# Adding the residual of an MLP block on TensorE instead of VectorE and GpSimd

## The chip, the cores and the metric

The kernel runs on one core of one Trainium2 chip. The metric is the device time of one execution in microseconds, as the median of several runs. The engines appear in the rows as PE (TensorE, with PEld for its weight loads), DVE (VectorE), ACT (ScalarE), POOL (GpSimd) and SP (SyncE, which issues the DMAs).

## The reference

The input is 8 batches of 576 tokens, 8 heads of 64 elements (512 channels). Cut to what matters:

```python
attn = softmax(blockmask(q @ k.T / 8)); x = heads_joined(attn @ v)
h = x.transpose(0, 2, 1) @ U @ V                 # mixes tokens, rank 32
u = x + h.transpose(0, 2, 1)
y = u + np.maximum(u @ w_ch1, 0.0) @ w_ch2       # 512 -> 2048 -> 512
gate = sigmoid(causal_conv5(y)); out = gate * (y @ w_val) @ w_out
```

The change concerns the `u +` in the line of `y`.

## The kernel before

Products run in fp32r. To keep the accuracy of fp32, an operand is held as a high half and a low half (`uh`, `ul`; `w1hi`, `w1lo`; `hh`, `hl`), and a product is three matmuls: high by high, low by high, high by low. The helper `hi_act` (recorded at L89) rounds a tile to its high half on ACT, `lo` (recorded at L95) subtracts to get the low half on DVE or POOL.

The 4608 tokens are cut into 9 groups g of 512 columns. The MLP of a group runs in 16 slices f of the 2048 hidden channels, so one step is s = (g, f). `emit_h1` makes a slice of the hidden layer (12 matmuls at L824 into one PSUM bank, then `hh` by a relu on ACT at L852 and `hl` on DVE at L853). `emit_o` multiplies the slice by its rows of w2 (12 matmuls at L870, three for each of the four 128-channel blocks d) and adds them up over the 16 slices in four PSUM banks, `acc[0..3]`, which stay taken for the whole group. `emit_o` of a step stands after `emit_h1` of the next one. The other four PSUM banks are shared by everything else: attention scores, products with v (`pPV`, L595), the mixing and the hidden layer.

When f = 15 is done, the group's result is taken out, for each d: DVE adds `uh` to the bank (L882), POOL adds `ul` (L883), SP stores the 128x512 block to DRAM (L884). The tile `y` comes from a pool of two buffers, so the third block of a group needs the first block's store to have landed. From group 7 on other tiles are used, eight buffers of `gt`. The sums of the last group and its gate run at the end.

The attention of later batches is woven into the MLP steps. A generator yields pieces of it; `gap()`, called at fixed places in `emit_h1` and `emit_o`, runs as many pieces as the pace asks for. Among them are the mixing steps for a pair of heads: `mix_T` transposes x (`pT`, four 128-column products at L655, one of 64 rows at L663), `mix_G` multiplies by U (`pG`, L671), `mix_H` multiplies by V (`pH`, L694), adds the result to x on DVE (`xt`, L696) and writes the halves of u for a later group (`uh` on ACT, `ul` on POOL).

The halves of u have two buffers. Group g + 2 takes the buffer of group g, so `mix_H` puts a piece for group g + 2 into the list `later` until `y_done` has reached g. `flush_later` takes one piece from that list; it is called right after `y_done` is set, and in every second `gap()`.

The order of the work on PE is the one in which the program writes it (PE is scheduled by hand). The order on ACT, DVE, POOL and SP is set by the tile scheduler when the kernel is built; work under `tc.high_priority()` is put ahead. Each engine then runs its list in that order.

Of the kernel before, what the change touches and what calls it, by code (L numbers as in the profile page):

```python
# [9 lines left out]
F32R = mybir.dt.float32r  # L10
# [3 lines left out]
ALU = mybir.AluOpType  # L14
# [3 lines left out]
P = 128  # L18
# [4 lines left out]
def attn_moe_gate_kernel(ctx: ExitStack, tc: tile.TileContext, q, k, v, U, V, w1, w2, wval, convw, wout, out):  # L23
# [8 lines left out]
    ND = DM // P  # L32
    NF = DFF // P
# [49 lines left out]
    def f32(ap):  # L83
        return ap if ap.dtype == F32 else ap.bitcast(F32)

    vec, act, pool, pe, sp = nc.vector, nc.scalar, nc.gpsimd, nc.tensor, nc.sync
# [60 lines left out]
    const = ctx.enter_context(tc.tile_pool(name="const", bufs=1, side="left"))  # L147
# [13 lines left out]
    def open_mlp_psum():  # L161
        first.close()
        psum["acc"] = mlp.enter_context(tc.tile_pool(name="accp", bufs=1, space=PSUM, side="left"))
# [54 lines left out]
    ident = ac_p.tile([P, P], F32, name="ident")  # L218
    make_identity(nc, ident)
    unit = const.tile([KC, KC], F32, name="unit")  # L220
    pool.tensor_copy(unit, ident[0:KC, 0:KC])

    w1hi = w1_p.tile([P, ND, DFF], F32R, name="w1hi")
    w1lo = w1_p.tile([P, ND, DFF], F32R, name="w1lo")
# [393 lines left out]
    ut = {}  # L618
# [8 lines left out]
    def mix_pieces(b):  # L627
        t0, t1 = b * S, (b + 1) * S
        r = []
        for g, (a, n) in enumerate(groups):  # L630
            lo_t, hi_t = max(a, t0), min(a + n, t1)
            if lo_t < hi_t:
                r.append((g, lo_t - t0, hi_t - t0, lo_t - a))
        return r
# [46 lines left out]
    def mix_H(pn, i):  # L681
        pcs = mix_pieces(pn // NP)
        if i >= len(pcs):
            return
        gi, a0, a1, off = pcs[i]
        if gi >= 2 and gi > y_done[0] + 2:
            later.append((pn, i))
            return
        xt = xts[pn]
        d = pn % NP  # L690
        uh, ul = u_tiles(gi)
        w = a1 - a0
        ps = ps_p.tile([P, 512], F32, tag="a", name="pH")
        pe.matmul(ps[:, 0:w], gst[pn], vst[:, a0:a1], start=True, stop=True)  # L694
        with tc.high_priority():
            vec.tensor_tensor(xt[:, a0:a1], ps[:, 0:w], xt[:, a0:a1], op=ALU.add)  # L696
        hi_act(uh[:, d, off:off + w], xt[:, a0:a1])
        lo(pool, ul[:, d, off:off + w], xt[:, a0:a1], uh[:, d, off:off + w])

    def flush_later():  # L700
        if later and mix_pieces(later[0][0] // NP)[later[0][1]][0] <= y_done[0] + 2:
            mix_H(*later.pop(0))

    y_done = [-1]
# [111 lines left out]
    accs = {}  # L816

    def h1_sum(ps, s, d):
        g, f = divmod(s, NF)
        n = groups[g][1]  # L820
        uh, ul = ut[g]
        fs = slice(f * P, (f + 1) * P)
        for i, (w, x) in enumerate(((w1hi, uh), (w1hi, ul), (w1lo, uh))):
            pe.matmul(ps[:, 0:n], w[:, d, fs], x[:, d, 0:n], start=(d == 0 and i == 0), stop=(d == ND - 1 and i == 2))  # L824
# [12 lines left out]
    def emit_h1(s, gap):  # L837
        g, f = divmod(s, NF)
        n = groups[g][1]
        if s in h1p:  # L840
            ps = h1p.pop(s)
            h1_sum(ps, s, ND - 1)
        else:
            ps = psum["h1"].tile([P, GS], F32, tag="a" if psum["h1"] is ps_p else "h1", name="h1")
            for d in range(ND):
                h1_sum(ps, s, d)
                if d == 1:
                    gap()
        hh = h_p.tile([P, GS], F32R, tag="hh", name="hh")
        hl = h_p.tile([P, GS], F32R, tag="hl", name="hl")  # L850
        with tc.high_priority():
            act.activation(hh[:, 0:n], ps[:, 0:n], AF.Relu)  # L852
            latest[0] = vec.scalar_tensor_tensor(hl[:, 0:n], ps[:, 0:n], 0.0, f32(hh[:, 0:n]), op0=ALU.max, op1=ALU.subtract)  # L853
        gap()
        hts[s] = (hh, hl)

    def emit_o(s, gap):
        g, f = divmod(s, NF)
        t0, n = groups[g]
        if f == 0:  # L860
            if g == 0:
                open_mlp_psum()
            accs[g] = [psum["acc"].tile([P, GS], F32, tag=f"acc{d}", name=f"acc{d}") for d in range(ND)]
        acc = accs[g]
        hh, hl = hts.pop(s)
        w = w2t.pop(s)
        for d in range(ND):
            ds = slice(d * P, (d + 1) * P)
            for i, (wi, x) in enumerate(((0, hh), (0, hl), (1, hh))):
                pe.matmul(acc[d][:, 0:n], w[:, wi, ds], x[:, 0:n], start=(f == 0 and i == 0), stop=(f == NF - 1 and i == 2))  # L870
            if d == 1:
                gap()
        gap()
        if f == NF - 1:
            uh, ul = ut.pop(g)
            ys = []
            for d in range(ND):
                if pbp and g < NG - 1:
                    y = pbp["g"].tile([P, GS + HALO], F32, tag="gt", name="gt")
                else:  # L880
                    y = late["y"].tile([P, GS], F32, tag="y", name="y")
                vec.tensor_tensor(y[:, 0:n], acc[d][:, 0:n], f32(uh[:, d, 0:n]), op=ALU.add)  # L882
                pool.tensor_tensor(y[:, 0:n], y[:, 0:n], f32(ul[:, d, 0:n]), op=ALU.add)  # L883
                sp.dma_start(out=y_s[g][:, d, :], in_=y[:, 0:n])  # L884
            y_done[0] = g
            flush_later()


    wv = {}
# [110 lines left out]
    def open_pb():  # L1000
        att.close()
        split.close()
        pbp["w"] = pb1.enter_context(tc.tile_pool(name="pbw", bufs=1, side="right"))
        pbp["g"] = pb1.enter_context(tc.tile_pool(name="pbg", bufs=GBUF, side="right"))
        pbp["y1"] = pb1.enter_context(tc.tile_pool(name="pby1", bufs=1, side="right"))
        open_stage("right", 2)
        load_conv()
        load_wb(pbp["w"])
        stage.close()
        pbp["y2"] = pb1.enter_context(tc.tile_pool(name="pby2", bufs=1, side="right"))  # L1010
        if ABUF == 4:
            psum["h1"] = pb1.enter_context(tc.tile_pool(name="h1p", bufs=2, space=PSUM, side="right"))
        pbp["ps"] = pb1.enter_context(tc.tile_pool(name="pbps", bufs=2, space=PSUM, side="right"))
# [32 lines left out]
    def gap():  # L1046
        tick_count[0] += 1
        if tick_count[0] % EVERY == 0:
            flush_later()
        pace[0] += pace[1]  # L1050
        while pace[0] > 0 and pace[2] == 0:
            pace[0] -= 1.0
            r = next(stream, 2)
            if r:
                pace[2] = r
                if r == 2:
                    while later:
                        flush_later()
                    open_pb()

    gated_conv[0] = GATE0
    for s in range(NS + LAG):
        g, f = divmod(s, NF)
# [5 lines left out]
        if f == 0 and g < B:  # L1069
            while g > 0 and not pace[2]:  # L1070
                pace[0] = 1.0
                gap()
            if g > 0:
                emit_o(s - LAG, gap)
            if pace[2] != 2:
                pace[2] = 0
            aim(g)
        if s < NS:
            if g == NG - 1:
                if f == 1:  # L1080
                    load_y(0)
                    split_tiles(0, pbp["y1"])
                    load_y(1)
            if cwt:
                wait_conv[0] -= 1
                if not wait_conv[0]:
                    turn_conv()
            emit_h1(s, gap)
            load_w2(s)
            if g == NG - 1 and 4 <= f < 4 + 2 * ND:  # L1090
                g_, d = divmod(f - 4, ND)
                if g_ == 0:
                    split_y(0, d)
                emit_gate(g_, d)
        if s >= LAG and not (f == 0 and g < B):
            emit_o(s - LAG, gap)
# [54 lines left out]
```

## Time and profile before

| | before |
|---|---|
| median of 3 runs | 1516.54 us (1515.33 to 1517.08) |
| the profiled execution, its own time | 1518.09 us |
| span of the profiled execution | 1516.3 us |
| mean granted TensorE clock | 0.977 of 2.4 GHz |
| busy: PE, DVE, ACT, POOL | 94%, 72%, 46%, 23% of the span |

The span goes from the first to the last instruction of the profiled execution; its own time holds 1.8 us around it. That execution lies 1.55 us over the median of the runs. In rows of the timeline the first number is the start and the second the duration; matmuls are pipelined, so that the time that one costs PE is the distance from its start to the next start, and not its duration. A bracket at the end of a row is the idle time of the engine just before, and what ended it.

### The profile page before, as it was taken

Reading aid. Unit: us, or ns where it says so; the run is one execution under the profiler, and the core shown is the slowest. Engines: PE = TensorE matmul, PEld = TensorE weight load, DVE = VectorE, ACT = ScalarE, POOL = GpSimd, SP = SyncE. Lnnn points to the kernel's source line nnn. Section 1 sums busy time; section 2 is a strip of 40 time slices with the busy share of each in tenths; the row PEclk is TensorE's granted clock in tenths of the full one; section 3 lists DMA queues with packets and bytes.
Section 4 is the critical chain, followed back from the end, with each engine's and each line's share of the span. In section 5 each row is a group of like instructions: output and inputs, shape, how many; then the busy total and the mean of one; then the engine's idle time right before and its main releaser. Section 6 shows DMA issues by size and latency. Waiting matters only on the chain.

```text
span 1516.3 us, 20089 instructions
## 1 busy us (share of the span) xinstructions
PE 1430.9 (94%) x6664; PEld 1106.4 (73%) x6664; DVE 1088.6 (72%) x2249; ACT 703.7 (46%) x1501; POOL 349.0 (23%) x449
## 2 busy tenths in 40 slices
PE   5889899979998998999899989999999999999999
PEld 3556667667776776777677767767888888778887
DVE  7778877677787888788777878887424427399991
ACT  4676555535544554456355445544413211244432
POOL 2123333121113112211311131122014210352410
PEclk9999899989999999999999999999999999999999
DMA  6445765333342434333333424421225533213211
GB/s 121 103 100 160 229 188 177 85 103 84 94 105 82 103 90 114 87 93 84 103 83 94 97 90 97 95 93 62 88 97 195 180 125 125 98 65 102 84 70 70
DMA packets 246289, 163.56 MB, mean 108 GB/s; under 512 B 197669, under 2 KB 212261, under 8 KB 246186
## 3 DMA queue, kind: packets, MB, share of 16 engines
q1 hardware_dynamic: 246186, 162.29, 37.7%
q8 instruction: 53, 0.87, 0.2%
q14 instruction: 50, 0.41, 0.1%
HBM read 134.98 MB, written 27.26 MB: 107 GB/s over the span
## 4 chain that ended last, share of the span: by engine, by line
PE 76%; DVE 15%; ACT 3%; DMA 2%; issue 2%; SPq 1%; POOL 1%; DVEq 0%; ACTq 0%; POOLq 0%
PE h L824 23%; PE acc L870 23%; PE pPV L595 8%; PE o L987 7%; PE pS L379 6%; PE val L963 5%; DVE rq L423 1%; DMA raw<-in_moe_w_ch_dram 1%; PE pG L671 1%; DVE s L510 1%; DVE y L882 1%; DVE wa L123 1%; DVE m L474 1%; PE pS L414 1%; DVE r L484 1%
## 5 line engine op out<-in xcount | busy, mean ns | idle before, releaser
L870 PE MATMUL acc<-hh,w 128*128 128x512 f32 x1152 | 405.4, 407 | 0.0
L870 PEld LDWEIGHTS acc<-hh,w 128*128 128x128 f32 x1152 | 220.4, 191 | 68.5 <-issue 22.5
L824 PE MATMUL h<-uh,w1hi 128*128 128x512 f32 x576 | 242.6, 421 | 2.6 <-ACT s L438 1.7
L824 PE MATMUL h<-uh,w1lo 128*128 128x512 f32 x576 | 229.5, 398 | 0.0
L824 PE MATMUL h<-ul,w1hi 128*128 128x512 f32 x576 | 229.0, 398 | 0.0
L870 PE MATMUL acc<-hl,w 128*128 128x512 f32 x576 | 227.8, 396 | 0.0
L853 DVE SCALAR_TENSOR_TENSOR hl<-h,hh 128x512 fp32r<-128x512 f32 x144 | 98.5, 684 | 132.9 <-ACT hh L852 131.5
L852 ACT ACTIVATE hh<-h 128x512 fp32r<-128x512 f32 x144 | 85.9, 597 | 188.9 <-PE h L824 182.3
L824 PEld LDWEIGHTS h<-uh,w1hi 128*128 128x128 f32 x576 | 110.6, 192 | 45.7 <-issue 21.7
L95 POOL TENSOR_TENSOR vlo<-vstk,vhi 128x320 fp32r<-128x320 f32 x46 | 43.1, 936 | 372.2 <-ACT vhi L89 353.4
L824 PEld LDWEIGHTS h<-uh,w1lo 128*128 128x128 f32 x576 | 110.3, 191 | 24.9
L870 PEld LDWEIGHTS acc<-hl,w 128*128 128x128 f32 x576 | 110.5, 192 | 20.5 <-issue 1.2
L824 PEld LDWEIGHTS h<-ul,w1hi 128*128 128x128 f32 x576 | 110.8, 192 | 19.8 <-issue 1.4
L945 DVE SCALAR_TENSOR_TENSOR gt<-yb,cw,gt 128x516 f32<-128x516 f32 (+1 forms) x144 | 116.5, 840 | 1.4
L379 PE MATMUL pS<-tq,tk 64*128 64x320 f32 (+4 forms) x552 | 92.4, 429 | 1.7 <-ACT s L384 1.7
L95 POOL TENSOR_TENSOR yl<-yb,yh 128x512 fp32r<-128x512 f32 (+7 forms) x64 | 67.7, 1091 | 97.6 <-ACT yh L89 97.4
L95 POOL TENSOR_TENSOR ul<-xt,uh 128x512 fp32r<-128x512 f32 (+7 forms) x64 | 54.0, 850 | 123.8 <-ACT uh L89 123.3
L384 ACT COPY s<-pS 128x512 f32<-128x512 f32 (+2 forms) x124 | 58.2, 496 | 48.5 <-PE pS L379 47.2
L596 ACT COPY xt<-pPV 64x128 f32<-64x128 f32 (+1 forms) x128 | 50.1, 392 | 65.6 <-PE pPV L595 63.8
L532 ACT ACTIVATE s<-s 128x448 f32<-128x448 f32 (+1 forms) x62 | 44.1, 711 | 73.6 <-DVE s L510 73.5
L510 DVE TENSOR_TENSOR s<-s,mb 128x64 f32<-128x64 f32 (+4 forms) x155 | 71.4, 524 | 0.3
L379 PEld LDWEIGHTS pS<-tq,tk 64*128 64x128 f32 x552 | 42.1, 185 | 35.8 <-issue 21.9
(163 smaller groups left out, 2810.9 us busy)
## 6 DMA issues: line engine op xcount, KB each, us to landing
w<-w_s SPq DMA_DIRECT2D x144, 512.0 KB, 3.2
rawq<-in_q_dram SPq DMA_DIRECT2D x128, 72.0 KB, 2.7
rawk<-in_k_dram SPq DMA_DIRECT2D x128, 72.0 KB, 2.9
out_dram<-ot SPq DMA_DIRECT2D x35, 256.0 KB, 2.0
vstk<-in_v_dram SPq DMA_DIRECT2D x64, 128.0 KB, 2.8
raw<-in_moe_w_ch_dram SPq DMA_DIRECT2D x64, 128.0 KB, 2.7
raw<-in_moe_w_ch_dram SPq DMA_DIRECT2D x16, 512.0 KB, 4.1
w_s<-wo SPq DMA_DIRECT2D x16, 512.0 KB, 3.3
```

The costliest lines, as they stand in the source:

```text
L95: eng.tensor_tensor(o, i, f32(h), op=ALU.subtract)
L379: pe.matmul(t[:, o:o + w], tk[me, kslice(j)], tq[me, a0:a1], start=True, stop=True)
L384: act.copy(stt[n][half_of[j]][:, d:d + o], t[:, 0:o])
L510: noted(3, vec.tensor_tensor(sv(n, j), sv(n, j), mb[:, q0[j]:], op=ALU.subtract))
L595: pe.matmul(o_, l_, r_, start=(i == 0), stop=(i == len(todo) - 1))
L824: pe.matmul(ps[:, 0:n], w[:, d, fs], x[:, d, 0:n], start=(d == 0 and i == 0), stop=(d == ND - 1 and i == 2))
L852: act.activation(hh[:, 0:n], ps[:, 0:n], AF.Relu)
L853: latest[0] = vec.scalar_tensor_tensor(hl[:, 0:n], ps[:, 0:n], 0.0, f32(hh[:, 0:n]), op0=ALU.max, op1=ALU.subtract)
L870: pe.matmul(acc[d][:, 0:n], w[:, wi, ds], x[:, 0:n], start=(f == 0 and i == 0), stop=(f == NF - 1 and i == 2))
L945: vec.scalar_tensor_tensor(gt[d][:, 0:gw], y[:, d, j:j + gw], cw[:, d, j:j + 1], gt[d][:, 0:gw], op0=ALU.mult, op1=ALU.add)
L963: pe.matmul(ps[:, 0:n], w[:, d, es], x[:, d, 0:n], start=(i == 0), stop=(i == 3 * ND - 1))
L987: pe.matmul(ps[:m, cs], x[:, e, a:a + m], w[:, e, cs], start=(i == 0), stop=(i == 3 * ND - 1))
```

## The change

A fp32r identity `identr` is made once on POOL. At f = 0 of a group, `emit_o` begins each of the four sums with two products with the identity, one of `uh` and one of `ul`, so 8 for a group and 72 in all; the products with w2 follow with `start=False`. At f = 15 the block is copied from PSUM by ACT (L890 of the changed kernel, under high priority) and stored. The 36 adds on DVE and the 36 on POOL are gone. Since u isn't needed at the end of the group any longer, `y_done` and the first `flush_later` move into `emit_h1`, behind the last slice's relu: ahead of the w2 products of f = 14 and f = 15, and not behind them.

```diff
+    identr = const.tile([P, P], F32R, name="identr")
+    pool.tensor_copy(identr, ident)
...
             latest[0] = vec.scalar_tensor_tensor(hl[:, 0:n], ps[:, 0:n], 0.0, f32(hh[:, 0:n]), op0=ALU.max, op1=ALU.subtract)
+        if f == NF - 1:
+            y_done[0] = g
+            flush_later()
         gap()
...
             accs[g] = [psum["acc"].tile([P, GS], F32, tag=f"acc{d}", name=f"acc{d}") for d in range(ND)]
+            for d in range(ND):
+                for i, u in enumerate(ut[g]):
+                    pe.matmul(accs[g][d][:, 0:n], identr, u[:, d, 0:n], start=(i == 0), stop=False)
...
-                pe.matmul(acc[d][:, 0:n], w[:, wi, ds], x[:, 0:n], start=(f == 0 and i == 0), stop=(f == NF - 1 and i == 2))
+                pe.matmul(acc[d][:, 0:n], w[:, wi, ds], x[:, 0:n], start=False, stop=(f == NF - 1 and i == 2))
...
-            uh, ul = ut.pop(g)
-            ys = []
+            ut.pop(g)
...
-                vec.tensor_tensor(y[:, 0:n], acc[d][:, 0:n], f32(uh[:, d, 0:n]), op=ALU.add)
-                pool.tensor_tensor(y[:, 0:n], y[:, 0:n], f32(ul[:, d, 0:n]), op=ALU.add)
+                with tc.high_priority():
+                    act.copy(y[:, 0:n], acc[d][:, 0:n])
                 sp.dma_start(out=y_s[g][:, d, :], in_=y[:, 0:n])
-            y_done[0] = g
-            flush_later()
```

PE, in the first slice of the group after the boundary g = 1, before: a mixing product `pH` stands just ahead of the transposes `pT` of another pair of heads, and the fifth transpose (L663) waits for DVE: for the `xt` add (L696) of that `pH`, which reads the PSUM bank that the transpose is to have.

```order
L824 MATMUL h_4488<-uh,w1lo 128x512
L694 MATMUL pH<-vst,g 128x192 [waits DVE_49]
L655 MATMUL pT<-ident,xt 128x128 [waits PE_49,Activation_49]
L655 MATMUL pT<-ident,xt 128x128 x3
L824 MATMUL h_4568<-uh,w1hi 128x512 [waits PE_49,Activation_49]
L824 MATMUL h_4568<-ul,w1hi 128x512
L824 MATMUL h_4568<-uh,w1lo 128x512
L824 MATMUL h_4568<-uh,w1hi 128x512
L824 MATMUL h_4568<-ul,w1hi 128x512
L824 MATMUL h_4568<-uh,w1lo 128x512
L663 MATMUL pT<-ident,xt 64x128 [waits DVE_49]
```

PE at the same place in the changed kernel (its lines are numbered by 2 higher here). The last of the four `pH` has gone ahead of the w2 products of f = 15; the fifth transpose (L665) waits for ACT, for the copy `lt` (L599) of the second `pPV` bank.

```order
L826 MATMUL h_4513<-uh,w1lo 128x512
L657 MATMUL pT<-ident,xt 128x128 [waits DVE_49]
L657 MATMUL pT<-ident,xt 128x128 x3
L826 MATMUL h_4588<-uh,w1hi 128x512 [waits PE_49,Activation_49]
L826 MATMUL h_4588<-ul,w1hi 128x512
L826 MATMUL h_4588<-uh,w1lo 128x512
L826 MATMUL h_4588<-uh,w1hi 128x512
L826 MATMUL h_4588<-ul,w1hi 128x512
L826 MATMUL h_4588<-uh,w1lo 128x512
L665 MATMUL pT<-ident,xt 64x128 [waits PE_49,Activation_49]
```

In the changed kernel three of the pieces of u stand before the w2 products of f = 14 and one before those of f = 15; what the transpose waits for is no longer on DVE but on ACT.

ACT at the same boundary, before: the copies of the two `pPV` banks (`xt`, `lt`), the casts for the next products, and the relu `hh` of the first slice of the next group.

```order
L596 COPY xt<-pPV 64x128 [waits PE_49]
L597 COPY lt<-pPV 64x128 [waits Activation_49]
L89 CAST eh<-s_4028 128x448 [waits PE_49]
L89 CAST eh<-s_4029 128x768 [waits PE_49]
L547 ACTIVATE ef<-s_4028 128x384 [waits PE_49]
L596 COPY xt<-pPV 64x448 [waits PE_49]
L597 COPY lt<-pPV 64x448
L89 CAST vhi<-vstk_151 128x5x64 [waits DMAHW7_49,DMAHW6_49,Pool_49]
L852 ACTIVATE hh<-h_4488 128x512 [waits PE_49,Activation_49]
L532 ACTIVATE za<-za 128x448 [waits DVE_49,Activation_49]
L89 CAST x<-pT 128x4x128 [waits PE_49]
L532 ACTIVATE zb<-zb 128x768 [waits DVE_49,Pool_49]
```

ACT in the changed kernel, from the second of the four copies of `y` on (the first stands just ahead). The waits for DMAHW2 and DMAHW3 of the third and fourth copy are for the landing of the first and second block's store, whose buffers they write.

```order
L89 CAST uh<-xt 128x192 [waits DVE_49]
L890 COPY y<-acc_3248 128x512 [waits PE_49]
L890 COPY y<-acc_3249 128x512 [waits DMAHW2_49,PE_49,Activation_49]
L890 COPY y<-acc_3250 128x512 [waits DMAHW3_49,PE_49,Activation_49]
L598 COPY xt<-pPV 64x128 [waits PE_49]
L599 COPY lt<-pPV 64x128
L89 CAST eh<-s_4042 128x448 [waits PE_49]
L89 CAST eh<-s_4043 128x768 [waits PE_49]
L549 ACTIVATE ef<-s_4042 128x384 [waits PE_49]
L534 ACTIVATE za<-za 128x448 [waits DVE_49]
L598 COPY xt<-pPV 64x448 [waits PE_49]
L599 COPY lt<-pPV 64x448
```

The copies of the `pPV` banks stand behind all four copies of `y`, and the copy `lt` of the second bank also behind the first exponential (L534), which waits for DVE.

## Rows read from the trace of the kernel before

**Rows 1.** Page part 1, busy time of each engine, whole span.

```profile
PE 1430.9 (94%) x6664; PEld 1106.4 (73%) x6664; DVE 1088.6 (72%) x2249; ACT 703.7 (46%) x1501; POOL 349.0 (23%) x449
```

**Rows 2.** Page part 4, the chain that ended last, by engine.

```profile
PE 76%; DVE 15%; ACT 3%; DMA 2%; issue 2%; SPq 1%; POOL 1%; DVEq 0%; ACTq 0%; POOLq 0%
```

**Rows 3.** Waits of PE for DVE before pT: us in total, times, longest us.

```profile
PE pT L663 <- DVE xt L696: 29.1, 5, 6.1
...
PE pT L655 <- DVE xt L696: 7.9, 1, 7.9
```

**Rows 4.** Chain of waits, twelve products of L870 in a row: start us, us, what.

```profile
365.64 2.72 PE acc L870 x12
```

**Rows 5.** Timeline of PE, boundary g=1: start us, us, what, count [idle before].

```profile
455.13 0.40 PE L870 MATMUL acc<-hh,w 128*128 128x512 f32 x1
...
468.72 0.42 PE L663 MATMUL pT<-ident,xt 128*64 128x128 f32 x1 [5.93 <-DVE xt L696]
...
469.37 0.63 PE L824 MATMUL h<-ul,w1hi 128*128 128x512 f32 x1
...
471.07 0.63 PE L824 MATMUL h<-uh,w1lo 128*128 128x512 f32 x1
...
471.66 0.61 PE L870 MATMUL acc<-hh,w 128*128 128x512 f32 x1
472.11 0.39 PE L870 MATMUL acc<-hl,w 128*128 128x512 f32 x1
```

**Rows 6.** Stretches of boundary g=1: busy us of PE, PEld, DVE, ACT, POOL; clock; DMA.

```profile
447.00:468.70 21.70, 15.78 (x76) 12.97 (x76) 21.25 (x40) 8.24 (x18) 7.10 (x8) 0.92 0.53 143
468.70:472.10 3.40, 3.38 (x9) 2.75 (x10) 2.65 (x7) 0.91 (x4) 2.21 (x3) 0.51 0.20 77
```

**Rows 7.** Timeline of DVE, boundary g=1.

```profile
454.91 1.27 DVE L492 TENSOR_TENSOR r<-r,r 64x18 f32<-64x18 f32 x1
...
457.07 1.15 DVE L494 COPY r<-r 32x18 f32<-32x18 f32 x1
...
461.54 0.13 DVE L492 TENSOR_TENSOR r<-r,r 64x18 f32<-64x18 f32 x1
...
467.72 0.68 DVE L882 TENSOR_TENSOR y<-acc,uh 128x512 f32<-128x512 f32 x1
468.32 0.34 DVE L696 TENSOR_TENSOR xt<-pH,xt 128x192 f32<-128x192 f32 x1
```

**Rows 8.** Timeline of POOL, boundary g=1.

```profile
454.67 1.48 POOL L883 TENSOR_TENSOR y<-y,ul 128x512 f32<-128x512 f32 x1 [3.55 <-DVE y L882]
456.86 1.34 POOL L883 TENSOR_TENSOR y<-y,ul 128x512 f32<-128x512 f32 x1 [0.71 <-DVE y L882]
```

**Rows 9.** Timeline of PE, boundary g=0.

```profile
326.58 1.12 PE L655 MATMUL pT<-ident,xt 128*128 128x128 f32 x4 [7.92 <-DVE xt L696]
...
327.93 0.63 PE L824 MATMUL h<-ul,w1hi 128*128 128x512 f32 x1
```

**Rows 10.** Timeline of DVE near the end.

```profile
1319.63 0.69 DVE L882 TENSOR_TENSOR y<-acc,uh 128x512 f32<-128x512 f32 x1 [3.37 <-DMA y_s<-y]
```

**Rows 11.** Timeline of PE near the end.

```profile
1322.27 0.48 PE L963 MATMUL val<-yh,wvh 128*128 128x512 f32 x1 [1.29 <-DVE gf L967]
...
1332.23 0.47 PE L963 MATMUL val<-yh,wvh 128*128 128x512 f32 x1 [1.33 <-DVE gf L967]
```

**Rows 12.** Page part 5, ACT copies from PSUM: count, busy us, mean ns.

```profile
L384 ACT COPY s<-pS 128x512 f32<-128x512 f32 (+2 forms) x124 | 58.2, 496 | 48.5 <-PE pS L379 47.2
```

**Rows 13.** The line of the y stores, L884: issue to landing.

```profile
DMA to landing us min/median/max: 2.3/3.1/7.0
```

**Rows 14.** Timeline of ACT, boundary g=1.

```profile
457.28 0.26 ACT L596 COPY xt<-pPV 64x128 f32<-64x128 f32 x1 [6.59 <-PE pPV L595]
...
460.56 0.53 ACT L597 COPY lt<-pPV 64x448 f32<-64x448 f32 x1
...
464.57 0.58 ACT L532 ACTIVATE za<-za 128x448 f32<-128x448 f32 x1 [2.50 <-DVE za L510]
```

## The prediction

> **What bounds the kernel now.** I read the busy times, the chain of waits, the waits of PE, and then the timeline of each engine at a group boundary. PE is busy for 94% of the span and makes up 76% of the chain that ended last; DVE makes up 15% [rows 1, 2]. So work added to PE costs its full time, unless it fills a gap, and the gaps of PE are worth finding. The waits name them: before a transpose `pT` PE waits for DVE's `xt` six times, 29.1 + 7.9 = 37.0 us in all [rows 3]. The six lie at the boundaries g = 0 to 5, one each; boundaries 6 and 7 have none.
>
> Products of 512 columns in an unbroken row take 2.72 us for twelve, 0.227 us each [rows 4]. At g = 1 the reader is to see that PE stands still for 5.93 us and then starts slowly: behind the gap the products start every 0.425 us (469.37 to 471.07, four distances) [rows 5]. The granted clock of that stretch is 0.51, the lower of the two levels (1.2 and 2.4 GHz), after the idle time [rows 6]. DVE, in contrast, is busy for 21.25 us of the 21.70 that end with the gap [rows 6]: it is the queue that PE waits for. In that queue stand the four adds of `y`, the last one just ahead of the awaited `xt` [rows 7]. Two tiny operations there take 1.27 and 1.15 us, where the first kind takes 0.13 us a little later [rows 7]; both lie on top of POOL's adds of `y` [rows 8].
>
> **What the change removes.** The fifth transpose no longer waits for `xt`: all four mixing pieces stand ahead of the last w2 products, and their adds come before DVE's queue gets long. The 37.0 us of stalls go, if nothing else is late. The slow start behind each goes with them. At g = 1 six products take 0.2 us too long each, and a small one and the first w2 product (471.66 to 472.11) 0.4 us together [rows 5]: 1.6 us. At g = 0 the stall is longer, 7.92 us, and so is the slow start, four transposes and eleven products, one of which is shown [rows 9]: 2.7 us. Five times 1.6 and 2.7 are 10.7 us.
>
> DVE loses the four adds at about 0.6 us and the 2.1 us of stretching at each boundary, over 4 us. That isn't counted again; it is why I expect DVE not to be late for the next thing that PE takes from it, `hl` of the new group's first slice. `hl` started at the end of the last `xt` in this trace, 468.6 [rows 7]; 4 us sooner is 464.6, done at 465.3. PE began its wait at 468.72 - 5.93 = 462.8 [rows 5]; without the wait it asks for `hl` after six more products, eight identity products and one more, at 466.2.
>
> Near the end of the kernel the third block's add waits 3.37 us for a store to land [rows 10], and PE has two gaps of 1.29 and 1.33 us behind that work [rows 11]. The copies there go out without POOL's 1.3 us in the path, so I take off 2.0 us; the bounds are 0 and 3.2 us (both gaps with their slow starts).
>
> **What it adds.** 72 identity products of 512 columns. No product with an identity of this size is in the trace; the nearest row is the w2 product of the same shape and type, 2.72 us for twelve, 0.227 us each [rows 4]. That gives 72 x 0.227 = 16.3 us, all on the path, since PE is. The bounds are 0.227, because no row of that shape in an unbroken run is shorter, and the 0.425 us of the slow clock [rows 5] (30.6 us), if each boundary keeps a stall. I take the lower one, with the stalls gone.
>
> The Trainium skill, TensorE: Matmul & The Clock Gate, Back-to-back issue gap, puts a sustained product of 512 columns at about 131 ns. By that the 72 products would cost an estimated 9.4 us and the sum would be 6.9 us lower; the rows above show 0.227 us, so it isn't used.
>
> The making of `identr` is one small copy on POOL, idle for 77% of the span, some 200 us before its first use: nothing. ACT gets 36 copies of 128x512 from PSUM. The nearest rows are 0.50 us on average for copies of that kind, some of them narrower [rows 12]; DVE's adds took 0.68 [rows 7]. ACT is busy for 46% [rows 1], so 36 x 0.6 = 21 us cost nothing by themselves. Their place does matter.
>
> **The new wait.** ACT runs in order, and the third and fourth copy write the buffers of the first and second, so they wait for those stores to land. Behind them on ACT stand the copies `xt` and `lt` of both `pPV` banks, and the fifth transpose now waits for the second `lt`. At g = 1, in the times of this trace: the last of the twelve products of slice 15 starts at 455.13 [rows 5], eleven distances of 0.227 after the first, so the first bank is complete at 453.4, and copies one and two end at about 454.2 and 454.8. A store lands 2.3 / 3.1 / 7.0 us after its issue (minimum, median, maximum) [rows 13]. By the median, and with 0.2 us until the issue (an estimate), copies three and four end at 458.1 and 458.7. The work from the first `xt` to the second `lt` took from 457.28 to 461.09, 3.4 us of it busy, and an exponential of 0.58 us has come between [rows 14], so `lt` ends at 462.7. PE asks for it at 462.8: no stall, but no margin. From there each microsecond by which a store lands later is a microsecond of stall. The DMA engines are busy for 53% of this stretch, against 20% behind it [rows 6], so I take a landing of 4.2 us and not the median: a stall of 1.0 us, and 0.3 us, a fifth of the 1.6, for a start that may be slow. Six times 1.3 is 7.8 us. The bounds are 0, and at 7.0 us each time 3.8 + 1.6 = 5.4, 32 us.
>
> The other order of the lists on DVE, ACT and SP in the first 300 us, which the scheduler works out anew, I bound by 3 us to either side and take at nothing. SP's w2 loads keep their places; the y stores now stand 1.3 us earlier.
>
> **The sum.** -37.0 - 10.7 - 2.0 + 16.3 + 7.8 = -25.6 us. The profiled execution has a span of 1516.3 us and its own time of 1518.09 us; this makes it 1492.5. It lies 1.55 us above the median of the runs, so the median is forecast at 1516.5 - 25.6 = 1491 us.
>
> **The rivals.** Call S what each of the six boundaries still loses, slow clock included. The time is 1516.5 - 33.4 + 6 S = 1483 + 6 S.
>
> (1) *Nothing is late, S = 0: 1483 us.* For it: the median landing just suffices. Against it: the margin is zero, and DMA is busy there. The Trainium skill, DMA: Bandwidth & Descriptors, Anatomy of one DMA — SWDGE (gpsimd) path, fits a DMA (of that path) with 2.0 us and its bytes at 436 GB/s; that makes an estimated 2.6 us for a store of 256 KB, and this outcome. The median in [rows 13] is 3.1 us, half a microsecond more, and only the minimum is below.
>
> (2) *DVE stays the bound.* The stretching may come from POOL's other work as well, and the mixing adds only change places. If nothing is freed, `hl` ends at 469.2 where PE asks at 466.2: S = 3.0 + 1.6 = 4.6, 1511 us. With half of it freed, S is about 2.5: 1498 us. For it: DVE is busy for 98% of that stretch [rows 6]. Against it: four adds do leave its list.
>
> (3) *Slower than before: the stores.* If the landing holds ACT at every boundary, copies, `lt`, exponentials and relus all wait, and PE with them. The new kernel is level with the old one at S = 5.6. By the working above, S = (landing - 3.2) + 1.6 with the slow clock, so the stores have to land after 7.2 us at every boundary to be level, and after 7.7 us to be slower by the measure below. Landings of 9 us would give S = 7.4: 1527 us. Against it: 7.0 us is the longest of 36 stores. For it: the four stores of a group now come closer together, between loads of w2 and v.
>
> That the change doesn't do what it says is no case here: the order of PE's list shows that the wait for `xt` is gone.
>
> **How the numbers follow.** What a measurement of this kernel can tell from no change is about 0.2%, 3 us. The forecast (S from 0.5 to 2.2, 1486 to 1496 us, with 3 us to either side for the first 300 us) has a chance of 0.52. Rival 1 has 0.18; rival 2 has 0.18, from 1496 to 1512. The remaining 0.12 lies with the stores: 0.05 for S of about 5 to 6, within 0.2%, and 0.07 for slower. Faster is then 0.88. The range leaves out the lower half of rival 1 and the cases from 1510 us on: 1482 to 1510.
>
> **What would show it right or wrong.** In the changed kernel's waits, PE's wait for `xt` before `pT` should be gone, and a wait for ACT's `lt` of about 1 us, six times, should stand in its place. On ACT the third copy of `y` at a boundary should sit idle until the store has landed. 72 products at L871 should start 0.227 us apart. On DVE the tiny operations should be back at 0.2 us. The clock behind the boundary should stay at its upper level. I am wrong if PE waits for `hl` at the first slice of a group (rival 2), if ACT stands for more than 5 us at the third copy (rival 3), or if the granted clock falls to its lower level behind the new wait at every boundary.

## The result, and the profile after

| | before | after |
|---|---|---|
| median | 1515.93 us (4 runs) | 1477.53 us (1474.48 to 1478.79, 4 runs) |
| profiled execution: span, mean granted clock | 1516.3 us, 0.977 | 1476.2 us, 0.994 |

The ratio is 0.9746, with a 95% interval of 0.9726 to 0.9765: 38.4 us less, where 25.6 us were forecast. The time lies below the range (1482 to 1510). The page of the changed kernel, busy times and the chain by engine, answers to [rows 1, 2]:

```profile
PE 1431.2 (97%) x6736; PEld 1107.3 (75%) x6736; DVE 1046.3 (71%) x2213; ACT 720.6 (49%) x1537; POOL 297.6 (20%) x414
...
PE 84%; DVE 7%; DMA 3%; ACT 3%; issue 2%; SPq 1%; POOL 1%; DVEq 0%; ACTq 0%; POOLq 0%
```

PE's busy time is the same within 0.3 us, although 72 products were added: what the slow clock no longer costs pays for most of them, by the estimate below the table. The span is 40.1 us shorter, and DVE's share of the chain has fallen from 15% to 7%. The stretches of the boundary g = 1 (columns as in [rows 6]) show it in one place:

```profile
429.00:452.20 23.20, 23.20 (x110) 17.27 (x108) 18.71 (x44) 12.85 (x30) 6.90 (x13) 1.00 0.53 146
452.20:455.70 3.50, 3.46 (x17) 2.79 (x17) 3.40 (x9) 2.91 (x7) 0.88 (x1) 1.00 0.00 0
```

PE is busy without a gap that the profile counts (23.20 of 23.20 us, 3.46 of 3.50), the granted clock is 1.00 on either side of the transpose, where it was 0.51 behind the stall, and DVE has slack (18.71 of 23.20 us). PE's timeline there, answering to [rows 5]:

```profile
451.91 0.40 PE L826 MATMUL h<-uh,w1lo 128*128 128x512 f32 x1
452.35 0.30 PE L665 MATMUL pT<-ident,xt 128*64 128x128 f32 x1
452.40 0.48 PE L826 MATMUL h<-uh,w1hi 128*128 128x512 f32 x1
...
453.64 0.39 PE L826 MATMUL h<-uh,w1lo 128*128 128x512 f32 x1
453.87 0.39 PE L871 MATMUL acc<-uh,identr 128*128 128x512 f32 x1
...
455.46 0.39 PE L871 MATMUL acc<-ul,identr 128*128 128x512 f32 x1
455.69 0.39 PE L878 MATMUL acc<-hh,w 128*128 128x512 f32 x1
```

The fifth transpose starts 0.44 us behind the product before it, where 0.23 us would be the unbroken distance: a wait of 0.2 us in place of 5.93. The eight identity products take 455.69 - 453.87 = 1.82 us, 0.2275 us each. What the transpose waits for is seen on ACT:

```profile
443.27 0.59 ACT L890 COPY y<-acc 128x512 f32<-128x512 f32 x1 [1.75 <-PE acc L878]
...
444.30 0.58 ACT L890 COPY y<-acc 128x512 f32<-128x512 f32 x1
446.64 0.59 ACT L890 COPY y<-acc 128x512 f32<-128x512 f32 x1 [1.76 <-DMA y_s<-y]
448.10 0.59 ACT L890 COPY y<-acc 128x512 f32<-128x512 f32 x1 [0.88 <-DMA y_s<-y]
...
451.76 0.53 ACT L599 COPY lt<-pPV 64x448 f32<-64x448 f32 x1
```

The third copy of `y` waits for the first block's store, 1.76 us, the fourth for the second's, 0.88 us. The second `lt` (L599) starts at 451.76 and ends at 452.29; PE had asked for it at 452.14. So the new wait is there, with no margin and a loss of 0.2 us. The waits of the changed kernel, with the total, the times and the longest:

```profile
ACT y L890 <- DMA y_s<-y: 20.6, 12, 2.8
...
PE pT L665 <- ACT lt L599: 0.3, 1, 0.3
```

ACT waits 20.6 us for landings, as was expected of it; of the transposes one is listed, with 0.3 us (g = 0). The second profile, after_again, has 0.34 us at g = 0 and 0.19 us at g = 1, and nothing at the other four. The stores landed sooner than in [rows 13]:

```profile
DMA to landing us min/median/max: 2.3/2.9/4.6
```

On DVE the tiny operations that had been stretched [rows 7] are short again, one partly (beside a subtraction of POOL), and `hl` is done at 455.22, before PE asks for it at 455.91:

```profile
444.65 0.57 DVE L494 TENSOR_TENSOR r<-r,r 64x18 f32<-64x18 f32 x1
...
445.52 0.17 DVE L496 COPY r<-r 32x18 f32<-32x18 f32 x1
...
454.57 0.65 DVE L855 SCALAR_TENSOR_TENSOR hl<-h,hh 128x512 fp32r<-128x512 f32 x1
```

Near the end one gap of PE is left, of the two in [rows 11]:

```profile
1292.17 0.47 PE L968 MATMUL val<-yh,wvh 128*128 128x512 f32 x1 [0.79 <-DVE gf L972]
```

Where the time went is best read from the starts of the relu `hh` (ACT's timeline), here for two profiles of each kernel; the second ones come from the runs before_again and after_again below.

| from ... to | before | after | difference of the means | forecast |
|---|---|---|---|---|
| start to the first relu | 135.66, 133.51 | 134.15, 135.33 | +0.2 | |
| to slice 14 of group 0 | 162.18, 161.26 | 159.89, 159.49 | -2.0 | +1.8 |
| to slice 4 of group 7 (six boundaries with stalls, and g = 6) | 859.82, 861.85 | 823.37, 824.47 | -36.9 | -27.2 |
| to slice 15 of group 8 | 147.00, 147.03 | 149.25, 149.26 | +2.2 | +1.8 |
| to the end of the span | 211.64, 210.65 | 209.54, 209.55 | -1.6 | -2.0 |

The forecast's column deals out its own terms: stalls, slow clock and residual waits to the third line, and the identity products 8 to the second, 56 to the third and 8 to the fourth. The third line holds most of what was missed.

That line can be taken apart. PE's waits of over 0.1 us add up to 38.7 and 40.0 us there before, to 2.3 and 2.6 us after. PE is busy at the lower level of the clock for 29.4 and 31.2 us before, for 3.4 and 5.8 us after; with products every 0.425 us there and every 0.227 us at the upper level [rows 4, 5], 47% of that is lost, an estimated 13.7 and 14.6 us against 1.6 and 2.7 us. What is left is 807.4 and 807.3 us before, 819.5 and 819.2 us after. In the means this is -36.9 us by the waits, -12.0 us by the clock and +12.0 us for the 56 products.

### The profile page after: what moved, and what is told of

The parts are those of the page before. It is cut to its first block, busy times and chain, and to the rows that moved or that the text cites. A ratio compares the mean times of both kernels' runs of the same rounds, so it can differ in the third digit from the quotient of the medians.

```text
span 1476.2 us, 20134 instructions
## 1 busy us (share of the span) xinstructions
PE 1431.2 (97%) x6736; PEld 1107.3 (75%) x6736; DVE 1046.3 (71%) x2213; ACT 720.6 (49%) x1537; POOL 297.6 (20%) x414
## 4 chain that ended last, share of the span: by engine, by line
PE 84%; DVE 7%; DMA 3%; ACT 3%; issue 2%; SPq 1%; POOL 1%; DVEq 0%; ACTq 0%; POOLq 0%
PE acc L878 26%; PE h L826 25%; PE pPV L597 9%; PE o L992 7%; PE val L968 6%; PE pS L381 6%; DMA raw<-in_moe_w_ch_dram 2%; PE pS L416 1%; DVE wa L123 1%; PE acc L871 1%; PE pG L673 1%; PE pT L657 1%; DVE wa L141 1%; PE pE L456 1%; DVE rq L425 1%
## 5 line engine op out<-in xcount | busy, mean ns | idle before, releaser
L878 PEld LDWEIGHTS acc<-hh,w 128*128 128x128 f32 x1152 | 217.3, 189 | 67.7 <-issue 23.1
L826 PE MATMUL h<-uh,w1hi 128*128 128x512 f32 x576 | 238.3, 414 | 1.7 <-DVE xt L698 1.0
L826 PE MATMUL h<-uh,w1lo 128*128 128x512 f32 x576 | 226.2, 393 | 0.0
L826 PE MATMUL h<-ul,w1hi 128*128 128x512 f32 x576 | 225.5, 391 | 0.0
L826 PEld LDWEIGHTS h<-uh,w1hi 128*128 128x128 f32 x576 | 108.7, 189 | 44.3 <-issue 20.6
L534 ACT ACTIVATE s<-s 128x448 f32<-128x448 f32 (+1 forms) x62 | 44.0, 710 | 64.3 <-DVE s L512 64.0
L512 DVE TENSOR_TENSOR s<-s,mb 128x64 f32<-128x64 f32 (+4 forms) x155 | 65.1, 483 | 0.3
```

Of the source, the lines that this page charges most:

```text
L512: noted(3, vec.tensor_tensor(sv(n, j), sv(n, j), mb[:, q0[j]:], op=ALU.subtract))
L878: pe.matmul(acc[d][:, 0:n], w[:, wi, ds], x[:, 0:n], start=False, stop=(f == NF - 1 and i == 2))
```

## The experiments

Theory A: the order is what counts; the pieces of u stand a step sooner, so that no transpose waits for the last `xt`. Theory B: DVE's relief is what counts, and the order doesn't matter. The prediction had both: it took the stalls off by the order and used the relief only to say that nothing else would be late. late_flush, early_adds, dve_copy and half_id ran beside the kernel before at 1518.61 us (13 runs); no_pool, y1, zero72 and mix6 at 1517.71 us (8 runs); after_again and before_again at 1517.78 us (15 runs). Ratios are against these.

**late_flush**: everything of the change, but the order as before.

```diff
-        if f == NF - 1:
-            y_done[0] = g
-            flush_later()
...
                 sp.dma_start(out=y_s[g][:, d, :], in_=y[:, 0:n])
+            y_done[0] = g
+            flush_later()
```

> The changed kernel with y_done and the first flush_later back at the end of the group; identity products and ACT copies kept. Theory A (the order: the mixing pieces of u stand a step sooner, so that no transpose waits for the last xt): the waits of pT for xt come back six times, shortened by the 4.3 us that DVE no longer spends on the adds and the stretching, so some 1.6 us each and 1 us of slow clock, 16 us in all: about 1493 us. Theory B (DVE's relief alone; the order doesn't matter): no such wait, within 3 us of the changed kernel, 1478. Theory C (relief worth nothing): waits of over 5 us as before, plus the identity products: 1525 or more.

Measured: 1491.18 us, ratio 0.9824 (0.9794 to 0.9855). The time is theory A's, its reason isn't: no transpose waits for `xt` at all. The waits that are left are of hidden-layer products, for ACT's second `lt` (waits; then the copy and the product at g = 1):

```profile
PE h L826 <- ACT lt L599: 10.9, 6, 2.5
```
```profile
452.13 0.53 ACT L599 COPY lt<-pPV 64x448 f32<-64x448 f32 x1
```
```profile
452.71 0.49 PE L826 MATMUL h<-uh,w1hi 128*128 128x512 f32 x1 [1.49 <-ACT lt L599]
```

With the order as before the product behind the transposes takes the PSUM bank of that `lt`, six products earlier than the fifth transpose does in the changed kernel, so the same copy comes 1.5 to 2.5 us late. The relief alone brings 27 us, with the identity products paid; the order brings another 11.8 us (0.9824 against 0.9746; the two intervals together leave 6 to 17 us). From slice 14 of group 0 to slice 4 of group 7 late_flush takes 837.30 us, 13.4 us more than the changed kernel: by these waits, and by a slow clock behind those at g = 2 and 3 (granted clock 0.968 from slice 14 to slice 4 there, 1.00 in the changed kernel).

**early_adds**: the order of the change, with the adds left on DVE and POOL and no identity products.

```diff
+        if f == NF - 1:
+            y_done[0] = g
+            flush_later()
         gap()
...
-            y_done[0] = g
-            flush_later()
```

> The kernel before with only y_done and flush_later moved as in the change; the adds stay on DVE and POOL, no identity products. Theory A alone (the order is all): the six waits for xt and their slow clock go, 48 us, and no identity is paid: about 1468 us. Theory B (DVE must be relieved too): hl of the new group's first slice, at 468.6 in the trace before, comes 4 us after PE asks for it (464.4 without the wait), so waits of 3 to 4 us before acc's hl and 1.6 us of slow clock at six boundaries: 1498 to 1503 us.

Measured: 1518.21 us, ratio 0.9985 (0.9969 to 1.0001): nothing gained. The waits of PE for `hl`, six at the w2 products or the hidden layer of the boundaries 0 to 5 and a few small ones:

```profile
PE acc L873 <- DVE hl L853: 25.5, 6, 6.1
...
PE h L824 <- DVE hl L853: 8.5, 2, 7.8
```

The six are 7.76, 4.25, 6.08, 4.40, 5.77 and 4.27 us, 32.5 us in all, where the six for `xt` had been 37.0. DVE's timeline at g = 1 shows why:

```profile
459.14 1.27 DVE L492 TENSOR_TENSOR r<-r,r 64x18 f32<-64x18 f32 x1
...
461.30 1.15 DVE L494 COPY r<-r 32x18 f32<-32x18 f32 x1
...
469.68 1.12 DVE L494 COPY r<-r 32x18 f32<-32x18 f32 x1
470.83 0.69 DVE L885 TENSOR_TENSOR y<-acc,uh 128x512 f32<-128x512 f32 x1
471.44 0.68 DVE L853 SCALAR_TENSOR_TENSOR hl<-h,hh 128x512 fp32r<-128x512 f32 x1
```

DVE still carries the adds (L885) ahead of `hl`, and the small operations are again stretched to over 1.1 us. No transpose waits for `xt` any more, so the order alone does take that wait off; PE then waits for `hl`. This is rival 2 of the prediction in its purest form. Theory B named the wait, but its 1498 to 1503 us are 15 to 20 us too low: the wait is DVE's whole queue, and whichever product asks it first gets it.

**dve_copy**: the copies of `y` on DVE instead of ACT.

```diff
-                    act.copy(y[:, 0:n], acc[d][:, 0:n])
+                    vec.tensor_copy(y[:, 0:n], acc[d][:, 0:n])
```

> The changed kernel with the four copies of y on DVE instead of ACT. Then the wait for the store's landing stands in DVE's list. If DVE's place is what decides (theory B): 2.6 us of copies and up to 2.6 us of waiting put hl of the next group 4 us later, where it has about 1.3 us of margin: waits of 2 to 4 us and 1.6 us of slow clock at six boundaries, 1500 to 1512 us. If the order alone decides (theory A): 1478, within 3 us.

Measured: 1487.80 us, ratio 0.9785 (0.9761 to 0.9810), between the two theories:

```profile
DVE y L890 <- DMA y_s<-y: 5.2, 6, 2.0
PE acc L878 <- DVE hl L855: 4.9, 5, 1.5
```

DVE waits for landings too, 5.2 us in all, and `hl` is late by 0.5 to 1.5 us at five boundaries, where 2 to 4 us and a slow clock were expected. From slice 14 of group 0 to slice 4 of group 7 it takes 829.24 us, 5.3 us more than the changed kernel. Against early_adds the four operations of DVE are the same in number and length, and POOL's part is gone. But PE also runs eight identity products here before it takes `hl`, 1.8 us that early_adds doesn't have, so this pair doesn't set POOL's part apart. The next run does.

**no_pool**: the kernel before, without POOL's adds.

```diff
-                pool.tensor_tensor(y[:, 0:n], y[:, 0:n], f32(ul[:, d, 0:n]), op=ALU.add)
```

> The kernel before without POOL's adds; y lacks the low half of u, so that this computation is left out; DVE's adds, the order and the late flush stay. If POOL's adds cost DVE 2 to 4 us at each boundary by stretching what runs beside them: the six waits for xt fall from 6 to 2 to 4 us, 15 to 25 us less than before, 1492 to 1502. If the stretching has another cause: within 3 us of before.

Measured: 1499.34 us, ratio 0.9896 (0.9861 to 0.9932), 16 to 18 us less (10 to 21 us by the interval), although no instruction of DVE or PE was taken out. The waits of the transposes for `xt` are halved, some of `lt` come up, and the two operations of [rows 7] are back at 0.16 us:

```profile
PE pT L663 <- DVE xt L696: 15.8, 5, 4.0
...
PE h L824 <- ACT lt L597: 6.6, 4, 2.8
```
```profile
448.68 0.16 DVE L492 TENSOR_TENSOR r<-r,r 64x18 f32<-64x18 f32 x1
...
449.74 0.16 DVE L494 COPY r<-r 32x18 f32<-32x18 f32 x1
```

Busy times of the whole span:

```profile
PE 1422.5 (95%) x6664; PEld 1099.2 (73%) x6664; DVE 1066.9 (71%) x2249; ACT 703.9 (47%) x1501; POOL 305.8 (20%) x413
```

DVE's 2249 operations take 21.7 us less than the same 2249 before [rows 1]; 21.3 us of this lie between slice 14 of a group and slice 2 of the next one at the boundaries 0 to 5, 3.3 to 3.8 us at each. Stores that land earlier aren't the reason: DVE idled for a landing at none of these six boundaries before, and at all six without POOL's adds (0.5 to 2.8 us).

So the removal of POOL's 36 adds by itself brings nearly half as much as the whole change, and POOL is an engine that was busy for 23% of the span and for whose adds nothing on PE waited.

**half_id**: identity products for `uh` alone, `ul` added by POOL behind ACT's copy.

```diff
-                for i, u in enumerate(ut[g]):
+                for i, u in enumerate(ut[g][:1]):
...
+                pool.tensor_tensor(y[:, 0:n], y[:, 0:n], f32(ul[:, d, 0:n]), op=ALU.add)
                 sp.dma_start(out=y_s[g][:, d, :], in_=y[:, 0:n])
```

> The changed kernel with identity products for uh alone (36); POOL adds ul to y behind ACT's copy. If identity products cost 0.227 us each and POOL's adds lie off the path: 36 x 0.227 = 8 us less, 1469 to 1470 us. If POOL's adds stretch DVE's operations as in the trace before (2 us a boundary) and DVE is then late: nothing gained, 1477 to 1484. The store and its landing come 1.3 us later, so ACT's third copy as well: if that wait decides, six times 1.3 us and more, 1478 to 1486.

Measured: 1534.90 us, ratio 1.0102 (1.0082 to 1.0122): slower than either kernel, and outside all three expectations. 8 us of products are saved and over 60 lost:

```profile
PE acc L878 <- DVE hl L855: 32.6, 5, 7.7
...
PE h L826 <- DVE hl L855: 9.6, 1, 9.6
```

Six waits for `hl` of 5.8 to 9.6 us, 42 us without their slow clock. DVE and then POOL at g = 1:

```profile
458.11 1.21 DVE L492 COPY r<-r 64x18 f32<-64x18 f32 x1
459.35 1.53 DVE L476 TENSOR_TENSOR m<-m,s 128x320 f32<-128x320 f32 x1
...
468.06 3.16 DVE L95 TENSOR_TENSOR el<-s,eh 128x448 fp32r<-128x448 f32 x2
...
475.65 0.68 DVE L855 SCALAR_TENSOR_TENSOR hl<-h,hh 128x512 fp32r<-128x512 f32 x1
```
```profile
458.00 2.53 POOL L891 TENSOR_TENSOR y<-y,ul 128x512 f32<-128x512 f32 x2 [3.54 <-ACT y L890]
...
468.72 1.68 POOL L891 TENSOR_TENSOR y<-y,ul 128x512 f32<-128x512 f32 x1
470.48 1.73 POOL L95 TENSOR_TENSOR ul<-xt,uh 128x192 fp32r<-128x192 f32 x2
```

A copy and a maximum at the start, L492 and L476, take 1.21 and 1.53 us beside POOL's two adds (in the changed kernel the copy takes 0.17 us); the pair `el` takes 3.16 us beside POOL's fourth add (1.50 in the changed kernel). And u's buffer is read by POOL to the end, so the four `ul` subtractions for the next group come at 470.48, on top of DVE's last steps, and `hl` starts at 475.65. The scheduler has also put five of DVE's subtractions ahead of `hl`; the two causes weren't separated.

**y1**: one buffer for `y`.

```diff
-        late["y"] = lpool("yp", 2)
+        late["y"] = lpool("yp", 1)
```

> The changed kernel with one buffer for y in groups 0 to 6 instead of two, so that every copy of y after the first waits for the landing of the store before it. If ACT's place behind the landing is what the new transpose wait hangs on (the forecast's own mechanism): copies 2 to 4 each come a landing of 2.5 to 3 us and 0.6 us after the last, the fourth ends some 5 us later than in the changed kernel, lt too, and PE's wait grows from 0.2 to about 5 us, with 1.6 us of slow clock: six times 6.5, 39 us more, about 1517. If the scheduler moves the late copies behind lt: a wait at the w2 products or the identity products of the next group instead, for acc, of 0 to 3 us each: 1478 to 1496.

Measured: 1487.93 us, ratio 0.9812 (0.9780 to 0.9844). The second case: at g = 1 the scheduler has put the fourth copy behind `lt`, and PE waits only 0.27 us for `lt`:

```profile
448.54 0.59 ACT L890 COPY y<-acc 128x512 f32<-128x512 f32 x1 [2.60 <-DMA y_s<-y]
...
451.62 0.59 ACT L890 COPY y<-acc 128x512 f32<-128x512 f32 x1 [0.87 <-DMA y_s<-y]
...
453.53 0.53 ACT L599 COPY lt<-pPV 64x448 f32<-64x448 f32 x1
...
456.15 0.60 ACT L890 COPY y<-acc 128x512 f32<-128x512 f32 x1
```

The largest single loss is at g = 6, where the first identity product waits for the bank that ACT hasn't emptied:

```profile
1109.14 0.52 PE L871 MATMUL acc<-uh,identr 128*128 128x512 f32 x1 [3.94 <-ACT y L890]
```

So this run doesn't test the forecast's chain from a landing to `lt`, or the slope of rival 3 (a microsecond of stall for each microsecond of landing): made longer at build time, the wait moves elsewhere. Landings that are late at run time, with the list unchanged, weren't tried, and the slope isn't shown.

**zero72**: a second product with zeros behind each identity product.

```diff
+    zeror = const.tile([P, P], F32R, name="zeror")
+    pool.memset(f32(zeror), 0.0)
...
                     pe.matmul(accs[g][d][:, 0:n], identr, u[:, d, 0:n], start=(i == 0), stop=False)
+                    pe.matmul(accs[g][d][:, 0:n], zeror, u[:, d, 0:n], start=False, stop=False)
```

> The changed kernel with 72 more products of the identity's size, with a matrix of zeros, behind each identity product. Theory: each costs its 0.227 us wherever PE is the bound, 16.4 us in all, and nothing in group 0, whose products fall among waits (1.8 us): 14.5 to 16.4 us more, 1492 to 1494. If a product with an unchanged stationary operand of this kind costs less than the row of w2 products says, or fills gaps: 0 to 8 us more.

Measured: 1500.81 us, ratio 0.9895 (0.9864 to 0.9927), 21 to 23 us more than the changed kernel, not 16. Between relu starts from slice 14 of group 0 to slice 4 of group 7 it takes 836.81 us against 823.37 and 824.47: 12.9 us for 56 products, 0.230 us each, as expected; another 1.8 us for the eight of group 8. The rest lies ahead of slice 14 of group 0, which starts its relu at 304.05 us (294.04 and 294.82 in the changed kernel): 4 us of it before the first relu, and 5.5 us behind that, 1.8 us of it for the eight products there; the order of DVE's and ACT's lists differs there as well, and the rest wasn't taken apart.

**mix6**: six identity products for a group; DVE takes blocks 0 and 1 out and adds `uh` to them.

```diff
-                for i, u in enumerate(ut[g]):
+                for i, u in enumerate(ut[g][(1 if d < 2 else 0):]):
...
                 with tc.high_priority():
-                    act.copy(y[:, 0:n], acc[d][:, 0:n])
+                    if d < 2:
+                        vec.tensor_tensor(y[:, 0:n], acc[d][:, 0:n], f32(uh[:, d, 0:n]), op=ALU.add)
+                    else:
+                        act.copy(y[:, 0:n], acc[d][:, 0:n])
```

> The changed kernel with six identity products for a group instead of eight: the sums of blocks 0 and 1 begin with ul alone, and DVE takes these two out with the add of uh; blocks 2 and 3 stay as they are (ACT). If 0.227 us each and DVE's 1.2 us lie within its margin of 1.3 us ahead of hl: 18 x 0.227 = 4.1 us less, 1473 to 1474. If DVE's margin is used up: waits for hl of 0.5 to 1.5 us at six boundaries, 1476 to 1483.

Measured: 1481.14 us, ratio 0.9771 (0.9732 to 0.9810), no better than the change; 4.1 us of products are saved and given back where DVE is late:

```profile
PE acc L878 <- DVE hl L855: 4.0, 4, 1.8
```

Of the versions tried, none beats the changed kernel.

**after_again, before_again**: both kernels once more.

> The changed kernel once more, for a second profile of the same lists and a closer ratio. If the first 300 us gained nothing of their own and the 3.8 us by which the relu of slice 14 came sooner there are scatter between executions: that relu anywhere between 293 and 300 us, the boundaries as before (waits of 0.3 us or less before the fifth transpose), the ratio between 0.973 and 0.979. If the gain there belongs to the kernel: that relu at 294 us, within 1.

> The kernel before once more, for a second profile of the same lists: the ratio is 1. If the first 300 us are scatter: the relu of slice 14 between 293 and 301 us (297.8 in the trace before). The six waits for xt again at 5.5 to 8 us each.

Measured: the changed kernel 1479.78 us, ratio 0.9741 (0.9712 to 0.9769); the kernel before 1516.45 us, ratio 1.0005 (0.9982 to 1.0028). From group 1 on the boundaries repeat within 0.2 us for the changed kernel, and within 1.5 us for the one before (waits for `xt` of 7.92, 5.92, 5.85, 6.06, 5.62 and 5.62 us). The relu of slice 14 starts at 294.82 and 294.77 us: the 3.8 us by which it came sooner in the first profile are for the most part scatter. dve_copy and late_flush, whose lists are those of the changed kernel up to there, have it at 299.22 and 293.22. What scatters is the time to the first relu, 132.6 to 138.7 us; from there to slice 14 these four profiles of the changed lists need 159.5 to 160.6 us, and the four of the lists before (before, before_again, early_adds and no_pool) 161.0 to 162.8. So about 2 us are gained there all the same, with eight products more. The gain lies between the relus of slices 4 and 6 (27.17 and 26.35 us before, 22.91 and 23.11 after), where the scheduler's lists of DVE and ACT differ. Two waits of PE there, 4.43 us for `hl` and 1.97 us for `lt` before (4.36 and 2.15 in before_again), are 3.75 us for ACT's `mb` and 0.28 us for `lt` after (3.72 and 0.28): 2.4 of the 3.8 us. What in the lists shortens them wasn't traced further.

## Why the prediction was wrong

The sign and most terms held, the mechanism in part. The step that failed is "I take a landing of 4.2 us and not the median: a stall of 1.0 us": it added 7.8 us, and the runs show 0.2 to 0.3 us at two boundaries and nothing at the other four. At g = 1 the third copy starts 2.8 us after the first has ended, where the working by the median has 3.3 us (3.1, and 0.2 until the issue, which came 0.02 us behind the copy) and the figure taken 4.4. The working by the median (`lt` at 462.7, asked for at 462.8) was right within 0.3 us (452.29 and 452.14 after). The reason for the larger figure was the DMA share of the stretch; it was 0.53 after as well, and the median landing of the stores was 2.9 us and the longest 4.6 (2.8 and 4.6 in after_again). So rival 1 came true, with S near 0, and the time lies 5.5 us below its 1483 us. The estimate by the Trainium skill that stood beside it (DMA: Bandwidth & Descriptors, Anatomy of one DMA — SWDGE (gpsimd) path; 2.6 us) is nearer than 4.2 us, and under the measured median.

Point by point:

- Stalls, -37.0 us: right, all six are gone in both profiles.
- Slow clock, -10.7 us: about right, an estimated -12.0 us. At g = 1 to 5 the distance between the relus of equal slices fell by 5.7 to 6.5 us in the first pair of profiles; with 1.8 us of products added back that is 7.5 to 8.3 us, against stalls of 5.6 to 6.1 us and 1.6 us. At g = 0 the distance from slice 14 to slice 4 fell by 6.9 and 6.1 us, 8.7 and 7.9 us with the products, where 7.9 + 2.7 were forecast. A stretch at the lower level behind a wait for ACT's `s`, at some 297 to 301 us, is in both profiles after and in before_again, but not in the first profile before, so that this part is uneven between the pairs. From 302 us on the granted clock is 1.00 to the end in both profiles after.
- Why they go: half right. "The fifth transpose no longer waits for `xt`: all four mixing pieces stand ahead" is true of the list, and in early_adds the order alone does end that wait; but PE then waits for `hl`, 32.5 us in place of 37.0, and nothing is gained. late_flush, without the order, loses no time to `xt` either. So the time is gained by DVE's shorter queue, which the prediction used only as cover for `hl`: the -37.0 us came out, but not by the order to which they were put down. The order comes second, by the 11.8 us between late_flush and the change.
- The stretching by POOL's adds, "the 2.1 us of stretching at each boundary": its existence was right, its size too small. Without these adds DVE's operations take 3.3 to 3.8 us less at each boundary, and no_pool gains 16 to 18 us.
- Identity products, 0.227 us each: right (0.2275 in the trace, 0.230 from zero72, 0.21 from the 12.0 us for 56 above). The trace speaks against the 131 ns of the Trainium skill (TensorE: Matmul & The Clock Gate, Back-to-back issue gap) for these products. The eight of group 0 aren't seen in the time, since that stretch got shorter by more.
- First 300 us, "3 us to either side": not quite held in the mean, since the stretch to slice 14 came out at -2.0 us with eight products in it that the forecast had as +1.8 us. Taking it at nothing cost the forecast most of these 3.8 us, although the time to the first relu scatters by more.
- End of the kernel, -2.0 us: -1.6 us; one of two gaps went.

From -25.6 us to -38.1 us (the mean of two profiles each) the table leads by 3.8 us in the second line and 9.7 us at the boundaries, 7.8 us of these by the residual wait that didn't come, less 1.0 us in the other lines. The remaining 1.9 us at the boundaries are, by the parts of the third line, the slow clock (12.0 us where 10.7 were forecast) and the 56 products (12.0 us where 12.7 were forecast).

The range failed because it was cut at rival 1 with nothing further gained ("The range leaves out the lower half of rival 1"): 1482 us was one outcome with hardly any variation around it, and the 3 us set aside for the first part belonged below it as well.

## What to carry to other kernels

A queue that is busy from end to end is the cause of a wait, not the instruction in it that happens to be named; test this by asking what the next product would wait for if the named wait were gone. A lightly loaded engine can be the expensive one, if what it does stretches the operations of the engine that bounds a stretch. Where a new wait comes out at zero margin with measured durations, forecast it so, and put the doubt into the range, on both sides.

## What the runs showed of the hardware

POOL's adds of two SBUF tiles stretch what DVE runs beside them: a DVE operation of 0.13 to 0.17 us that starts beside one ends when the add ends (454.91 + 1.27 = 456.18 against 454.67 + 1.48 = 456.15; 457.07 + 1.15 = 458.22 against 456.86 + 1.34 = 458.20) [rows 7, 8]. The Trainium skill, SBUF — State Buffer, Who interferes with whom, says that DVE and GpSimd share a pair of ports, which one of them holds for a whole instruction while the other waits; a DVE instruction with two SBUF inputs is concerned, and a copy if it runs in a mode that uses both ports. The traces agree for the maxima (L492 [rows 7]) and for the subtractions L510, which take 8.5 us less in no_pool over the six boundaries; the copies L494 [rows 7] and L492 (half_id) are held in the same way, though the profile doesn't show their mode. What I hadn't expected is the total: 16 to 18 us for 36 adds of 1.45 us each in the mean.

A fp32r product of 512 columns with an identity costs PE the same as one of w2, 0.2275 us [rows 4], and ACT took a 128x512 block out of PSUM in 0.58 to 0.59 us, DVE in 0.67 to 0.69 us (dve_copy).

The time to the first relu scatters by 6 us between executions with the same lists (132.6 us in late_flush, 138.7 in dve_copy), while two executions of the changed kernel agree within 0.2 us for each group from group 1 on.
